# Linear attention and a gated feed-forward: one chunk more projected by block products, with the sums of its right operands on GpSimd

## The chip, the cores and the metric

One core of a Trainium2 chip runs the kernel. Its engines work side by side, each through its own list of instructions in order: TensorE (PE; its weight loads are PEld), VectorE (DVE), ScalarE (ACT), GpSimd (POOL) and SyncE (SP), which here issues the transfers. The metric is the time of one execution in microseconds on the device.

## The reference

```
q_s = softmax of q over the head's 64 columns
k_s = softmax of k over the 576 tokens of a sequence
kv  = einsum('bhsd,bhse->bhde', k_s, v)
x   = einsum('bhsd,bhde->bhse', q_s, kv), laid out as 4608 tokens x 512
out = ((x @ w_a) * (x @ w_b)) @ w_out        # w_a, w_b: 512 x 1536, w_out: 1536 x 512
```

Eight batches, eight heads, all in fp32.

## The kernel before, in words

The 4608 tokens are cut into nine chunks of 512 (`c` from 0 to 8). For each, the attention part makes x, and the feed-forward part two products, the gate (`a * b`) and the projection to the output. An fp32 product is made of three matmuls of parts: each operand is split into a high and a low part (`split` and the like: ScalarE casts the high part, VectorE subtracts it for the low one), and high x high, high x low and low x high are summed.

The 1536 columns of the gate are taken in NI = 6 pairs of blocks (`p`, and `i = pair_at(c, p)`, L1367, the pair that stands at place p). From chunk 1 on the gate of a pair goes by seven block products instead of eight (Strassen-Winograd): `product` (L848) makes each of 12 matmuls of 256 columns (L854) with weights that are sums of weight blocks (S1 to S4 and A11, A12, A22, 512 KB each), loaded again for each chunk by `get_w` (L493, SP). `last_w` keeps the weights of a chunk's last pair where the next chunk begins with the same pair.

The projection of chunks 0 to 2 is direct: `project` (L878), 144 matmuls of 512 columns for a chunk (L883), summed over all pairs in four banks, then `store`. Chunks 3 to 8 (`BY_BLOCKS = 3`) project by seven block products too: `block_step` (L1505) makes one of them, six matmuls of 256 columns (L1518). Its left operands are sums of gate blocks (`left_sums`, L1476, on VectorE), split by `split_lefts` (ScalarE L1471, VectorE L1472). Its right operands come from w_out by `right_sums(i)` (L1412), once for a pair: two sums of 512 columns (L1425) and four differences of 256 (L1431) on VectorE into y2 and t2, which are split into tiles `kept` (L1438, L1439). The kept tiles take the place of w_out's own tiles `wo`. The other right blocks are written to DRAM (`dr`) and come back through a ring of four slots by `get_right` (L1447). The pairs 0 to 4 have their right sums in chunk 2 (places 1 to 5), pair 5 at place 0 of chunk 3.

The keys of a batch are made ready by `kv_soft` (L530): VectorE takes maxima over the tile (L542 to L544, into m1), GpSimd a maximum over partitions (`partition_all_reduce`, L533, into mx), VectorE subtracts it (L565), ScalarE takes the exponential (L568), and TensorE multiplies keys and values (L603, into pk). Each is done twice for a chunk (two head groups). GpSimd also makes the sums of the gate's weights for chunk 1 (`sums`, L514).

The scheduler has no say: `ORDER` (L32) lists, for each engine, the order in which its instructions run, by their number in the program, and `in_order` (L294) makes a chain of them. An instruction that waits holds up all that stands behind it on its engine.

## Time and profile before

| | |
|---|---|
| median of 3 runs | 919.17 us (918.96 to 920.0) |
| the profiled execution | 917.98 us, span 916.2 us |
| TensorE busy | 904.6 us, 99% |
| VectorE busy | 714.4 us, 78% |
| ScalarE busy | 492.5 us, 54% |
| GpSimd busy | 113.2 us, 12% |
| moved through the SP queue | 305.16 MB |

The span is from the first to the last instruction of the profiled execution, and 1.8 us of its own time lie around it. Chunk 1 begins in the trace at 136.6 us, chunk 2 at 238.8, chunk 3 at 336.6, chunk 4 at 432.8. The page gives busy time over the whole span; how the stages differ is seen in the view by stretches, what an engine does one after the other in the timeline. The value in brackets behind a row of a timeline is how long the engine was idle just before, and who ended that.

### The profile page before, as it was taken

How to read it: one execution, taken by the hardware profiler on the slowest of the kernel's cores; microseconds unless marked ns; L12 is line 12 of the kernel's file. 1: busy time of each engine (PE TensorE's matmuls, PEld its weight loads, DVE VectorE, ACT ScalarE, POOL GpSimd, SP SyncE). 2: the span in 40 equal slices, each digit the busy share in tenths (PEclk: the TensorE clock that was granted, in tenths of full speed). 3: DMA queues.
4: the chain of work that ended last, by engine and by line, in shares of the span. 5: the costliest groups of instructions: out<-in, count | busy, mean ns of one | idle time of the engine just before them, and what ended most of it. 6: DMA issues, size and time to landing. Idle time of an engine off the chain costs nothing.

```text
span 916.2 us, 19531 instructions
## 1 busy us (share of the span) xinstructions
PE 904.6 (99%) x7155; PEld 850.2 (93%) x7155; DVE 714.4 (78%) x1557; ACT 492.5 (54%) x1350; POOL 113.2 (12%) x93
## 2 busy tenths in 40 slices
PE   7999999999999999999999999999999999999998
PEld 4677789899999999999999999999999999999997
DVE  7989999668966777679878887788877776876556
ACT  6989777555433456345735563446543655342322
POOL 3645343432100000000000000000000000000000
PEclk8999999999999999999999999999999999999999
DMA  9999999999999999999999989998999799959962
GB/s 350 380 384 367 378 369 363 365 362 341 385 350 329 361 338 322 393 322 346 333 346 350 331 301 352 324 356 306 343 323 399 247 349 326 385 189 320 347 252 93
DMA packets 124735, 306.40 MB, mean 334 GB/s; under 512 B 13408, under 2 KB 30432, under 8 KB 124640
## 3 DMA queue, kind: packets, MB, share of 16 engines
q1 hardware_dynamic: 124640, 305.16, 93.7%
q8 instruction: 57, 0.93, 0.4%
q14 instruction: 38, 0.31, 0.1%
HBM read 256.87 MB, written 48.23 MB: 333 GB/s over the span
## 4 chain that ended last, share of the span: by engine, by line
PE 89%; DMA 5%; ACT 2%; DVE 2%; issue 1%; SPq 0%; DVEq 0%; ACTq 0%
PE kx L854 30%; PE po L1518 19%; PE ky L854 15%; PE po L883 9%; PE ka L854 8%; PE pt L829 3%; PE px L785 2%; PE pk L603 2%; DMA raw<-in_w_ab 2%; DMA wo_raw<-in_w_out 1%; DMA dw<-ws 1%; DMA kt_first<-in_kt 1%; PE pl L1682 1%; DMA ws<-dw 1%; ACT wr L382 0%
## 5 line engine op out<-in xcount | busy, mean ns | idle before, releaser
L854 PE MATMUL kx<-xo,ws 128*128 128x256 f32 x2304 | 312.4, 282 | 0.0
L854 PEld LDWEIGHTS kx<-xo,ws 128*128 128x128 f32 x2304 | 292.1, 188 | 4.6 <-ACT u L1621 0.3
L854 PE MATMUL ky<-xo,ws 128*128 128x256 f32 x1152 | 157.7, 282 | 0.0
L854 PEld LDWEIGHTS ky<-xo,ws 128*128 128x128 f32 x1152 | 146.2, 188 | 0.9
L1472 DVE TENSOR_TENSOR left<-cc,left 128x256 fp32r<-128x256 f32 x245 | 96.2, 420 | 50.0 <-ACT left L1471 46.4
L1471 ACT CAST left<-cc 128x256 fp32r<-128x256 f32 x245 | 92.1, 404 | 65.8 <-DVE cc L1487 34.9
L1518 PE MATMUL po<-xo,left 128*128 128x256 f32 x750 | 106.2, 282 | 0.0
L1518 PE MATMUL po<-kept,left 128*128 128x256 f32 x720 | 100.7, 283 | 0.0
L1518 PEld LDWEIGHTS po<-xo,left 128*128 128x128 f32 x750 | 96.7, 189 | 0.4 <-issue 0.2
L1518 PEld LDWEIGHTS po<-kept,left 128*128 128x128 f32 x720 | 92.2, 189 | 0.4
L854 PE MATMUL ka<-xo,ws 128*128 128x256 f32 x576 | 80.7, 282 | 0.2 <-DMA ws<-dw 0.2
L696 ACT ACTIVATE qt<-qt,st 128x64 f32<-128x64 f32 x224 | 76.1, 342 | 6.9 <-issue 3.5
L829 PE MATMUL pt<-xo,ws 128*128 128x512 f32 x288 | 77.5, 407 | 0.1
L854 PEld LDWEIGHTS ka<-xo,ws 128*128 128x128 f32 x576 | 74.2, 188 | 1.7 <-DMA ws<-dw 0.6
L1621 ACT COPY u<-kx 128x512 f32<-128x512 f32 x48 | 28.2, 587 | 80.1 <-PE kx L854 39.1
L533 POOL PARTITION_ALL_REDUCE mx<-m x20 | 17.0, 849 | 423.0 <-DVE m L544 423.0
L829 PEld LDWEIGHTS pt<-xo,ws 128*128 128x128 f32 x288 | 53.0, 189 | 14.4 <-issue 2.6
L1487 DVE TENSOR_TENSOR cc<-cc 128x256 f32<-128x256 f32 x140 | 56.9, 420 | 1.6
L883 PE MATMUL po<-wo_w,gh 128*128 128x512 f32 x192 | 57.2, 396 | 0.0
L1607 ACT COPY u<-kx 128x512 f32<-128x512 f32 x48 | 28.1, 586 | 50.5 <-PE kx L854 50.3
L1642 ACT COPY cc<-kx 128x256 f32<-128x256 f32 x48 | 17.8, 371 | 68.5 <-PE kx L854 68.5
L1622 DVE TENSOR_TENSOR cc<-ky,u 128x512 f32<-128x512 f32 x48 | 33.0, 688 | 20.6 <-ACT u L1621 16.7
(175 smaller groups left out, 1368.2 us busy)
## 6 DMA issues: line engine op xcount, KB each, us to landing
ws<-dw SPq DMA_DIRECT2D x277, 512.0 KB, 6.6
xo<-dr SPq DMA_DIRECT2D x125, 256.0 KB, 5.6
dw<-ws SPq DMA_DIRECT2D x42, 512.0 KB, 6.8
mr<-dq SPq DMA_DIRECT2D x112, 128.0 KB, 6.6
raw<-in_w_ab SPq DMA_DIRECT2D x24, 512.0 KB, 7.6
vt<-in_v SPq DMA_DIRECT2D x28, 325.0 KB, 6.5
qt<-in_q SPq DMA_DIRECT2D x32, 256.0 KB, 5.1
kt<-in_k SPq DMA_DIRECT2D x24, 320.0 KB, 5.1
```

Source lines behind the costliest of these rows:

```text
L603: nc.tensor.matmul(pk[h * D:(h + 1) * D], kt[:, j, h], vt[:, j, h], start=(j == 0), stop=(j == J - 1),)
L696: nc.scalar.activation(out=qt[:, j, h], in_=qt[:, j, h], func=AF.Exp, bias=st[:, h, 0, j:j + 1], accum_out=st[:, h, 1, j:j + 1],)
L829: nc.tensor.matmul(pt, w[:, wp], x[g][:, xp], start=(g == 0 and i == 0), stop=(g == NP - 1 and i == 2),)
L854: ins = nc.tensor.matmul(pt[:, n], w[:, n, wp, c], x[:, xp, c], start=(first and n == 0 and i == 0), stop=(i == 5), skip_group_check=True,)
L883: nc.tensor.matmul(po[t], a[:, ts], wo[f][:, w], start=(f == 0 and i == 0), stop=(f == NF - 1 and i == 2),)
L1471: nc.scalar.copy(out=a[:, 0], in_=cc[:, n, part])
L1472: nc.vector.tensor_tensor(out=a[:, 1], in0=cc[:, n, part], in1=a[:, 0].bitcast(F32), op=ALU.subtract)
L1487: nc.vector.tensor_tensor(out=o, in0=x, in1=y, op=op)
L1518: nc.tensor.matmul(pt[:, t], x.left[:, ap, t * P:(t + 1) * P], w[:, wp], start=(first and t == 0 and n == 0), stop=(n == 2), skip_group_ch ...
L1607: nc.scalar.copy(out=u2, in_=kx)
L1621: nc.scalar.copy(out=u4, in_=kx)
L1622: nc.vector.tensor_tensor(out=cc[:, 3], in0=ky, in1=u4, op=ALU.add)
```

## The change

Chunk 2 projects by blocks as well (`BY_BLOCKS = 2`). The right sums are made on GpSimd, and earlier: pairs 0 to 2 in chunk 1 (places 2 to 4), pairs 4, 5 and 3 at the head of chunk 2 (places 0 and 1). The pairs run in reverse in every even chunk from chunk 2 on; before, in chunks 4, 6 and 8. With that chunk 1 ends with the pair chunk 2 begins with, and chunk 2 with that of chunk 3, and seven weights are kept at either boundary. All five lists of `ORDER` are replaced. The changed kernel's lines are 6 further on (L533 becomes L539, L1425 L1431, L1431 L1437), from the end of the function some more.

```diff
@@ ORDER
...
     "Pool": (
...
-        "41 44-88 "
...
+        "95 97 96 98 107-108 101-104 106 105 109-124 "
     ),
@@
-    BY_BLOCKS = 3
+    BY_BLOCKS = 2
...
     def pair_at(c, p):
-        return NI - 1 - p if c >= BY_BLOCKS and (c - BY_BLOCKS) % 2 else p
+        return NI - 1 - p if c > 0 and c % 2 == 0 else p
@@ right_sums
-            nc.vector.tensor_tensor(
+            nc.gpsimd.tensor_tensor(
                 out=y[:, r].rearrange("p a b -> p (a b)"), in0=w[:, 0], in1=w[:, 1], op=ALU.add
             )
...
         for o, x, z in ((t1, b12, b11), (t2, b22, t1), (t3, b22, b12), (t4, b21, t2)):
-            nc.vector.tensor_tensor(out=o, in0=x, in1=z, op=ALU.subtract)
+            nc.gpsimd.tensor_tensor(out=o, in0=x, in1=z, op=ALU.subtract)
@@ operand
                 if op in (A11, A12, A22):
-                    return get_w(i, op)
-                w = split_w(sy[i][op])
-                put_w(i, op, w)
+                    w = get_w(i, op)
+                else:
+                    w = split_w(sy[i][op])
+                    put_w(i, op, w)
+                if p == NI - 1 and pair_at(c + 1, 0) == i:
+                    last_w[i, op] = w
                 return w
@@ the loop over pairs
             kz = ka
+            if c == BY_BLOCKS and p == 0:
+                right_sums(NI - 2)
+                run_pending()
+                right_sums(NI - 1)
+                for _ in range(4):
+                    get_right()
+            if c == BY_BLOCKS and p == 1:
+                right_sums(NI - 3)
             multiply(kx, A11, B11, True)
...
-            if c == BY_BLOCKS - 1 and p > 0:
-                right_sums(p - 1)
+            if c == BY_BLOCKS - 1 and 2 <= p < NI - 1:
+                right_sums(p - 2)
...
-            if c == BY_BLOCKS and p == 0:
-                right_sums(NI - 1)
-                for _ in range(4):
-                    get_right()
```

The lists themselves tell a reader nothing, so three places of the orders follow, of the program before and of the changed one. `x10` is ten of a kind in a row, brackets name the engines or queues that an instruction waits for.

GpSimd around the maxima of the keys, before: the last sums for the gate's weights (L514), then an ISA row without operands, then the maxima over partitions of chunks 2 and 3 (L533).

```order
L514 TENSOR_TENSOR ws_y_2558<-ws_y_2554,ws_y_2558 128x512 [waits DMAHW2_49,Pool_49]
L514 TENSOR_TENSOR ws_y_2554<-ws_y_2560,ws_y_2554 128x512 [waits Pool_49]
L514 TENSOR_TENSOR ws_y_2556<-ws_y_2556,ws_y_2554 128x512 [waits DMAHW5_49,Pool_49]
L533 ISA
L533 ISA mx_3017<-m1_3019 128x128 [waits DVE_49]
L533 ISA mx_3026<-m1_3028 128x128 [waits DVE_49]
L533 ISA mx_3281<-m1_3283 128x128 [waits DVE_49,Pool_49]
L533 ISA mx_3290<-m1_3292 128x128 [waits DVE_49,Pool_49]
```

In the changed kernel, the same stretch: the first difference of t2_2744 (pair 2) stands ahead of the first two maxima, the rest of it and the sums of pairs 4 and 5 between them and the next two.

```order
L1437 TENSOR_TENSOR t2_2744<-y2_2743 128x256 [waits PE_49,Pool_49]
L539 ISA
L539 ISA mx_3153<-m1_3155 128x128 [waits DVE_49]
L539 ISA mx_3162<-m1_3164 128x128 [waits DVE_49]
L1437 ISA
L1437 TENSOR_TENSOR t2_2744<-y2_2743,t2_2744 128x256 [waits Pool_49]
...
L1437 TENSOR_TENSOR t2_3053<-y2_3052,t2_3053 128x256 [waits Pool_49] x2
L539 ISA
L539 ISA mx_3428<-m1_3430 128x128 [waits DVE_49]
L539 ISA mx_3437<-m1_3439 128x128 [waits DVE_49]
L1431 ISA
L1431 TENSOR_TENSOR y2_3324<-wo6_w_929 128x512 [waits DVE_49,Activation_49]
```

Where one row without operands stood in this stretch, four stand now, and 15 sums (four of 512 columns, eleven of 256) lie between the second and the third maximum. A fifth follows ahead of the maxima of chunk 4.

VectorE between the first maximum over partitions and the data of the second, before: from the subtraction of mx_3017 (L565) to the next maximum (L544), with the second subtraction at the end.

```order
L565 TENSOR_TENSOR kt_2940<-kt_2940,mx_3017 128x640
L802 TENSOR_TENSOR xt_2745<-xf_1587 128x512
L542 TENSOR_TENSOR m2_3027<-kt_2944 128x256
L543 TENSOR_TENSOR m1_3028<-m2_3027 128x128
L700 TENSOR_SCALAR st_2937<-st_2937 128x2x4
L1615 TENSOR_TENSOR cc_2763<-ka_2762,u3_2765 128x512
L544 TENSOR_TENSOR m1_3028<-m1_3028,kt_2944 128x128
```

In the changed kernel, the same stretch, from behind the subtraction of mx_3153 (kt_3012) to the maximum m1_3164 that the second all-reduce waits for.

```order
L1445 TENSOR_TENSOR kept10_2509<-t2_2496,kept10_2509 128x2x256
L366 TENSOR_TENSOR xo_2814<-xf_1587,xo_2814 128x512
L366 TENSOR_TENSOR gl1_2788<-cc_2582,gh1_2787 128x512
L1445 TENSOR_TENSOR kept11_2512<-t2_2496,kept11_2512 128x2x256
L983 TENSOR_TENSOR xf_1587<-px_2763,mr_2587 128x512
L548 TENSOR_TENSOR m2_3163<-kt_3016 128x256
L809 TENSOR_TENSOR xt_2818<-xf_1587,xt_2817 128x512
L814 TENSOR_TENSOR xt_2824<-xf_1587 128x512
L549 TENSOR_TENSOR m1_3164<-m2_3163 128x128
L707 RECIPROCAL st_3009<-st_3009 128x2x4
L706 TENSOR_SCALAR st_3009<-st_3009 128x2x4
L550 TENSOR_TENSOR m1_3164<-m1_3164,kt_3016 128x128
```

With the subtraction itself thirteen instructions stand between the two maxima, seven before.

TensorE where the keys of the next chunk are multiplied with their values, in chunk 2, before: pk_3377 stands behind the last direct projection of chunk 1 and ahead of gate products.

```order
L883 MATMUL po0_1742<-wo11_w_1513,gl1_2904 128x512
L883 MATMUL po2_1744<-wo11_w_1513,gl1_2904 128x512
L603 MATMUL pk_3377<-vt_3202,kt_3200 64x65 x10
L854 MATMUL kx_3181<-xo_2742,ws_3208 128x256 x12
L854 MATMUL ky_3182<-xo_2757,ws_3223 128x256 x12
L854 MATMUL kx_3181<-xo_2749,ws_3237 128x256 x12
L854 MATMUL ka_3183<-xo_2816,ws_3299 128x256 x6
L883 MATMUL po3_3096<-wo0_w_1522,gh0_3177 128x512 x2
```

In the changed kernel, that place: kt_3316 is the tile of keys that the third maximum, mx_3428, is subtracted from.

```order
L889 MATMUL po0_1742<-wo11_w_1513,gl1_2976 128x512
L860 MATMUL kx_3297<-xo_2826,ws_3470 128x256 x12
L860 MATMUL ka_3299<-xo_2888,ws_3446 128x256 x6
L860 MATMUL ky_3298<-xo_2829,ws_3366 128x256 x6
L609 MATMUL pk_3488<-vt_3318,kt_3316 64x65 x10
L1524 MATMUL po0_3380<-xo_3072,left_3278 128x256 x6
L609 MATMUL pk_3488<-vt_3322,kt_3320 64x65 x10
L1524 MATMUL po1_3403<-xo_3072,left_3279 128x256 x6
L1524 MATMUL po2_3462<-xo_3073,left_3280 128x256 x6
```

The block products of the projection (L1524) take the place of the direct ones in chunk 2, the first of them right behind pk_3488.

## Rows read from the trace of the kernel before

**Rows 1.** The page: busy time of each engine with its share of the span and its number of instructions (part 1), the granted clock of TensorE and the busy share of the DMA engines in tenths in 40 slices of the span (part 2), and the queue that SP feeds (part 3).

```profile
PE 904.6 (99%) x7155; PEld 850.2 (93%) x7155; DVE 714.4 (78%) x1557; ACT 492.5 (54%) x1350; POOL 113.2 (12%) x93
...
PEclk8999999999999999999999999999999999999999
DMA  9999999999999999999999989998999799959962
...
q1 hardware_dynamic: 124640, 305.16, 93.7%
```

**Rows 2.** The view by stretches, for chunks 1, 2 and 3: after the stretch and its length, the busy time of each engine with its instructions in brackets, in the order PE, PEld, DVE, ACT, POOL, then granted clock, DMA share and GB/s.

```profile
136.60:238.80 102.20, 102.05 (x781) 93.55 (x779) 80.90 (x170) 60.33 (x181) 34.24 (x24) 1.00 0.99 362
238.80:336.60 97.80, 97.80 (x729) 90.78 (x728) 71.99 (x146) 40.40 (x87) 3.40 (x4) 1.00 0.98 348
336.60:432.80 96.20, 96.20 (x835) 94.16 (x834) 75.91 (x179) 49.73 (x139) 3.41 (x4) 1.00 0.99 348
```

**Rows 3.** The tile ws, the weights of the gate's products: one of the lines on what its engines were idle for, with the time in us and the number of times.

```profile
  DMA ws<-dw: 0.7, 2
```

**Rows 4.** The timeline of TensorE in three short stretches of chunks 1 to 3: start, time from the first start to the last end of the group, line, operation, tiles, shape, number. Each group starts where the one before it has made its last start, so starts give the pitch.

```profile
237.45 1.39 PE L603 MATMUL pk<-vt,kt 128*64 128x65 f32 x40
238.76 1.10 PE L854 MATMUL kx<-xo,ws 128*128 128x256 f32 x7
...
245.15 1.55 PE L883 MATMUL po<-wo_w,gh 128*128 128x512 f32 x6
246.53 0.87 PE L883 MATMUL po<-wo_w,gl 128*128 128x512 f32 x3
247.24 0.88 PE L854 MATMUL kx<-xo,ws 128*128 128x256 f32 x6
...
358.98 2.30 PE L1518 MATMUL po<-xo,left 128*128 128x256 f32 x18
361.11 1.59 PE L854 MATMUL kx<-xo,ws 128*128 128x256 f32 x12
```

**Rows 5.** The groups of instructions by line and by form over the whole span: out<-in, shape, count, then busy us, mean ns of one, and the idle time before them with what ended most of it.

```profile
L1472 DVE TENSOR_TENSOR left<-cc,left 128x256 fp32r<-128x256 f32 x245 | 96.2, 420 | 50.0 <-ACT left L1471 46.4 <-PE ka L854 2.9
...
L1471 ACT CAST left<-cc 128x256 fp32r<-128x256 f32 x245 | 92.1, 404 | 65.8 <-DVE cc L1487 34.9 <-DVE cc L1623 12.1 <-PE po L1518 9.6
...
L514 POOL TENSOR_TENSOR ws_y<-ws_y 128x512 f32<-128x512 f32 x24 | 35.2, 1465 | 46.3 <-DMA ws_y<-dy 31.0 <-DVE xf L977 7.6 <-DMA mr<-dq 6.2
...
L568 ACT ACTIVATE kt<-kt 128x640 f32<-128x640 f32 x24 | 17.7, 738 | 18.8 <-DVE kt L565 17.8 <-DMA xo<-dr 1.0
...
L533 POOL PARTITION_ALL_REDUCE mx<-m x20 | 17.0, 849 | 423.0 <-DVE m L544 423.0
L360 DVE TENSOR_TENSOR gl<-cc,gh 128x512 fp32r<-128x512 f32 x24 | 16.9, 708 | 10.4 <-PE po L883 5.8 <-ACT gh L357 4.4
L360 DVE TENSOR_TENSOR xo<-xf,xo 128x512 fp32r<-128x512 f32 x24 | 16.6, 691 | 0.0
...
L565 DVE TENSOR_TENSOR kt<-kt,mx 128x640 f32<-128x640 f32 x20 | 16.3, 816 | 1.0 <-POOL mx L533 0.9
...
L360 DVE TENSOR_TENSOR ws<-wy,ws 128x512 fp32r<-128x512 f32 x18 | 16.0, 888 | 2.3 <-ACT ws L357 2.3
...
L1425 DVE TENSOR_TENSOR y<-wo_w 128x512 f32<-128x512 f32 x12 | 8.0, 684 | 0.0
...
L1431 DVE TENSOR_TENSOR t<-y,t 128x256 f32<-128x256 f32 x12 | 5.0, 420 | 0.1
```

**Rows 6.** The page's DMA issues: number, KB of each, and the median us from issue to landing.

```profile
ws<-dw SPq DMA_DIRECT2D x277, 512.0 KB, 6.6
xo<-dr SPq DMA_DIRECT2D x125, 256.0 KB, 5.6
```

**Rows 7.** The instructions of line 533 on GpSimd's queue: the row of the change of its configuration, with duration in ns, first and last start.

```profile
L533 POOLq MODIFY_POOL_CONFIG  x2: 13/13/13, 212.3 to 212.3; - x2
```

**Rows 8.** The same for line 1175, GpSimd's first sum of the run.

```profile
L1175 POOLq MODIFY_POOL_CONFIG  x2: 4/4/4, 1.5 to 1.5; - x2
```

**Rows 9.** The timeline of GpSimd around its last sums for the gate's weights and its first maximum over partitions.

```profile
205.26 6.80 POOL L514 TENSOR_TENSOR ws_y<-ws_y 128x512 f32<-128x512 f32 x4 [7.57 <-DVE xf L977]
224.13 1.05 POOL L533 PARTITION_ALL_REDUCE mx<-m  x1 [12.07 <-DVE m L544]
```

**Rows 10.** The timeline of VectorE from the maximum that the all-reduce of 224.13 waited for, and on into the stretch in which the second one is made ready.

```profile
223.71 0.29 DVE L544 TENSOR_TENSOR m<-m,kt 128x128 f32<-128x128 f32 x1
...
228.25 0.82 DVE L565 TENSOR_TENSOR kt<-kt,mx 128x640 f32<-128x640 f32 x1
228.98 0.69 DVE L802 TENSOR_TENSOR xt<-xf 128x512 f32<-128x512 f32 x1
231.15 0.43 DVE L542 TENSOR_TENSOR m<-kt 128x256 f32<-128x256 f32 x1 [1.48 <-DMA kt<-in_k]
...
233.29 0.68 DVE L977 TENSOR_TENSOR xf<-px,mr 128x512 f32<-128x512 f32 x1
233.90 0.68 DVE L1622 TENSOR_TENSOR cc<-ky,u 128x512 f32<-128x512 f32 x1
234.49 0.81 DVE L565 TENSOR_TENSOR kt<-kt,mx 128x640 f32<-128x640 f32 x1
```

**Rows 11.** The timeline of GpSimd at the start of the run.

```profile
10.48 1.05 POOL L1175 TENSOR_TENSOR qts<-qts,qst 128x512 f32<-128x512 f32 x1 [9.03 <-DVE qst L1169]
```

More of the change, by code (lines that the diff above doesn't have):

```diff
@@ L179 @@
         "70 98 79 100 93 137 92 99 103 101 138 80 102 112 95 220 116 113 109-111 153 108 119 117 128 120 "
[64 rows of a table removed]
[66 rows of a table added]
     ),
     "Pool": (
-        "0-7 10 12 8-9 11 13-16 18 17 19 21-22 24 20 25 23 27 26 28 30 29 31-34 36 35 37 40 39 38 42-43 "
-        "41 44-88 "
[3 rows of a table added]
     ),
```

463 rows, old and new, of the table ORDER are left out of this document.

## The prediction

> **What bounds the kernel now.** I read the page's busy times first. TensorE is busy for 99% of the span, at a granted clock of 0.9 or more in all slices but the first, which is the 2.4 GHz level [rows 1]. DMA is nearly as full, GpSimd has little to do. So the question is what TensorE has to do and where it could be made to wait. The stretches by chunk say the same of the place of the change: in chunk 2 (238.8 to 336.6) TensorE is busy for 97.80 of 97.80 us, and chunk 3, which already projects by blocks, takes 96.20 with more instructions [rows 2]. VectorE, 72 to 81 us of each, has room; a transfer of gate weights held TensorE up for 0.7 us in the whole run [rows 3]. A saving on TensorE is therefore a saving of time, as long as no new wait appears.
>
> **TensorE's own work.** In chunk 2, 144 matmuls of 512 columns (L883) go and 252 of 256 columns (L1518) come. From start to start, nine of L883 take 247.24 - 245.15 = 2.09 us, 0.2322 each; eighteen of L1518 take 361.11 - 358.98 = 2.13, 0.1183 each [rows 4]. 144 x 0.2322 = 33.4; 252 x 0.1183 = 29.8. **Saving 3.6 us.** The stretches of chunks 2 and 3 differ by 1.6 only, but they hold different amounts of attention work beside the products; I take the count.
>
> **VectorE and ScalarE.** Chunk 2 gains 42 left operands (ScalarE 42 x 404 ns = 17.0, VectorE 42 x 420 = 17.6), 24 sums of lefts (24 of the same width, 10.1) and some ten snapshots and sums of output banks (about 7.5, estimated at 0.7 each), and loses 12 low parts of gates (12 x 708 = 8.5) [rows 5]. Of the right sums' 18 us on VectorE (L1425 8.0 and L1431 in two halves of 5.0) five sixths, 15, lay in chunk 2 and go to GpSimd. VectorE there: 72.0 + 17.6 + 10.1 + 7.5 - 8.5 - 15 = 84 of some 94 us. ScalarE: 40 + 17 - 12 x 0.62 = 50. Both stay below TensorE, so this costs nothing; the cover is the ten us that VectorE is left with.
>
> **Transfers.** Fourteen loads of 512 KB go (the seven weights of a pair are kept at each of the two boundaries), 22 of right blocks of 256 KB come (18 for Q1 to Q3 and four for the first pair): 1.5 MB less of 305 [rows 1]. The SP queue is passed with no step later than a product needs it: ahead of each gate product in chunk 2 there are now fewer bytes, not more. I cost it at nothing; without that cover one late block costs its landing, 5.6 us [rows 6].
>
> **GpSimd.** It gets 12 sums of 512 and 24 of 256 columns. A 512 sum there takes 1465 ns on average [rows 5], a half one I estimate at 0.73, so 35 us, all in chunks 1 and 2, where it has 34 and 3 us of work [rows 2]. As throughput that is nothing. As a sequence it is the one thing that worries me. The first sum t2_2744 stands ahead of the all-reduces of the maxima of chunk 2's keys, the rest between those and the all-reduces of the next keys, and at each change of kind GpSimd's order has an ISA row without operands. The trace before has that twice: as MODIFY_POOL_CONFIG, 13 ns, at 212.3 ahead of the first all-reduce [rows 7], and at 1.5 ahead of the first sum [rows 8]. The changed order has three more on one chain. What such a **change of code, R,** costs before the first call can start isn't shown, since both times GpSimd had nothing to do anyway: the all-reduce of 224.13 starts 0.13 us after VectorE's maximum is done (223.71 + 0.29), the sum of 10.48 when VectorE releases it [rows 9, 10, 11]. That bounds R: at least 0, at most 10.48 - 1.5 = 9.0 (the other gap, 11.8, is wider). If R is anything, it is something brought in, and the nearest rows for that are the landings of transfers in these stretches, 5.6 to 6.6 us in a DMA system that is 0.98 to 1.00 busy [rows 2, 6]. I take **R = 7**, a little over the larger of these, and keep 0 and 9.0 for the range.
>
> The trace shows the first call itself starting 0.13 us after its input. The Trainium skill (GPSIMD Engine Reference, 2.1 Instruction dispatch) says that the first call to freshly loaded code pays about 6 us more, 5.95 measured, with no instruction to be seen, and to budget for it. That price is taken up under the second rival.
>
> The chain, from where TensorE finishes kx_2832's first product (t2_2744's first subtraction waits for it): that subtraction 0.73, R, all-reduce 0.85 [rows 5], then VectorE must do thirteen instructions in its order before the second maximum is complete. Seven are of 512 columns, 0.60 from start to start (233.29 to 233.90 to 234.49); the subtraction from the keys takes 0.73 (228.98 - 228.25), the three maxima 0.43 + 0.29 + 0.29, the two small ones about 0.1 each: 6.1, or 7.0 with nothing overlapped; I take 6.5 [rows 10]. Then the second all-reduce 0.85, R, four sums of 512 and eleven of 256: 4 x 1.465 + 11 x 0.73 = 13.9, R, all-reduce 0.85, VectorE's subtraction 0.82 (L565), ScalarE's exponential 0.74 (L568), and TensorE's pk_3488 may start. Sum: 0.73 + 0.85 + 6.5 + 0.85 + 13.9 + 0.85 + 0.82 + 0.74 = 25.2, plus 3R.
>
> TensorE's work between the same two points, counted in its order: 216 matmuls of the gate (256 columns), 52 of the direct projection, 20 of kv and six px: 216 x 0.1183 + 52 x 0.2322 + 20 x 0.033 (forty take 238.76 - 237.45 = 1.31) + about 0.9 = 39.3 [rows 4]. pk_3488 stands in TensorE's order ahead of the first block matmul; nothing behind it can pass. So the **new wait is 25.2 + 3R - 39.3 = 3R - 14.1**: none up to R = 4.7, 6.9 us at R = 7, 12.9 at 9.0. What queues behind it on VectorE are the lefts of pair 0, directly behind the two subtractions from the keys: they cost a fraction of a microsecond more, which I leave out. The first all-reduce has its own consumer, pk_3214, about 11 us of TensorE work after kx_2832 against 3.1 + R: no wait. The later switch, for pair 3's sums, has over 20 us.
>
> **Sum.** Against the profiled execution, 917.98 with a span of 916.2: -3.6 + 6.9 = +3.3, so 921.3. The median of the runs is 919.17, 1.19 higher, so **922.5**. A change under 0.2%, 1.84 us, can't be told from none; that makes 917.3 to 921.0 "no change", in R 5.3 to 6.5.
>
> **Rivals.**
> *The switches are short or early (the other side).* R is below 4.7, or the code is fetched while GpSimd still runs its sums. For it: in both switches of the trace the first call came straight after its input, and an instruction of 13 ns is all that is shown [rows 7, 9]. Against it: in both there were 9 to 12 us to hide in, and the new ones have none, since each stands between two pieces of ready work. Then only the saving is left: 919.17 - 3.6 = 915.6 (915.1 to 916.1, with the medians of single matmuls in place of the pitch). It decides at R = 5.9, where 3R - 14.1 is 3.6. Chance 0.28.
>
> *Draw.* R lies between 4.7 and 6, about the landings of 256 KB transfers: at 5.6 the wait is 2.7 and the time 918.3; from 915.6 to 919.5 over the case. Chance 0.16. By the 5.95 us of the Trainium skill (GPSIMD Engine Reference, 2.1) the wait would be 3.8 and the time 919.3; the trace so far neither shows such a price nor rules it out.
>
> *VectorE pays for GpSimd's sums.* VectorE's 512-wide instructions average 888 ns in the opening stretch, where GpSimd works too, against 691 later for the same width [rows 5]. At 30% more over the 35 us in which GpSimd is busy, VectorE has some 10 us more to do in two chunks with 94 and 102 us and 84 to 85 of work. Against it: TensorE ran through the stretches in which GpSimd did its sums for chunk 1 without a gap (102.05 of 102.20 busy, with 34 us of GpSimd) [rows 2]. Price: the backlog behind pk_3488 isn't made up, 3 us on top of the forecast, 925.5. Chance 0.04.
>
> *The rest comes late*: the block order's first right operands, four loads at the head of chunk 2, or kept tiles that wait for the old weights' last use. One landing, 5.6, in place of the stall: 921.2. Nor would the change then do what it says, save TensorE time. Chance 0.02.
>
> **Numbers.** The forecast, R from 6 to 9: 0.50; its own range 919.5 to 928.5, its likeliest time 922.5. Faster: the first rival and the draw up to R = 5.3, 0.28 + 0.05 = 0.33. Same: the rest of the draw, 0.11, and the forecast from 6 to 6.5, 0.06: 0.17. Slower: 0.44 + 0.04 + 0.02 = 0.50. The range must reach the first rival's 914.9 and R = 8.7 (3R - 14.1 = 12.0): 914.9 to 927.6.
>
> **What would show it.** In the changed profile: five more MODIFY_POOL_CONFIG stretches on GpSimd and gaps of about 7 us, with nothing released by another engine, on either side of the all-reduces near 225 and near 262; a hole in TensorE of about 7 us just ahead of L609 some 24 us into chunk 2, and no other hole; chunks 3 to 8 unchanged to a few tenths; 144 fewer L889 and 252 more L1524 at the same pitch. Wrong it would be if the gaps on GpSimd were under 5 us (then TensorE shows no hole and the end comes 3.6 earlier), or if the hole stood at a block matmul behind a left or a transfer.

## The result, and the profile after

The changed kernel takes **934.21 us** (932.43 to 935.21, 4 runs) where the kernel before, on the same chip, took 919.07: a ratio of **1.0147, 95% interval 1.0122 to 1.0171**, 15 us slower. 922.5 had been forecast, and 914.9 to 927.6 as the range. The profiled executions, 932.43 (span 930.6) and 917.98 (916.2), are apart by the same 14.4.

The page of the changed kernel, the lines of [rows 1], with the shares by engine of the chain that ended last (part 4):

```profile
PE 908.2 (98%) x7263; PEld 855.6 (92%) x7263; DVE 730.4 (78%) x1586; ACT 498.9 (54%) x1380; POOL 153.0 (16%) x129
...
q1 hardware_dynamic: 126304, 303.58, 92.3%
...
PE 75%; DMA 13%; DVE 6%; ACT 3%; issue 1%; SPq 1%; POOL 0%; DVEq 0%; ACTq 0%; POOLq 0%
```

TensorE holds the 108 more matmuls that were counted. In the kernel before the chain ran over TensorE for 89% and over transfers for 5%; now for 75% and 13%. Chunks 1 to 3 by stretches, as [rows 2] (after the length: PE, PEld, DVE, ACT, POOL, then granted clock, DMA share, GB/s):

```profile
133.70:247.30 113.60, 107.57 (x769) 95.97 (x768) 88.17 (x170) 64.91 (x201) 55.51 (x41) 0.98 0.96 345
247.30:347.40 100.10, 97.92 (x840) 94.11 (x839) 83.34 (x173) 51.40 (x133) 24.68 (x25) 1.00 0.97 338
347.40:445.70 98.30, 97.03 (x871) 96.00 (x871) 75.92 (x178) 44.49 (x122) 2.87 (x4) 1.00 1.00 348
```

Chunk 2 was to become shorter. Chunk 1 is 11 us longer, chunk 2 longer by 2, and even chunk 3, in which nothing was to change, by 2, with its transfers at a share of 1.00.

**The switches.** GpSimd around its all-reduces, where [rows 9] showed it in the kernel before:

```profile
224.17 0.73 POOL L1437 TENSOR_TENSOR t<-y 128x256 f32<-128x256 f32 x1 [2.72 <-PE kx L860]
234.43 0.72 POOL L539 PARTITION_ALL_REDUCE mx<-m  x1 [9.53 <-issue]
241.20 1.06 POOL L539 PARTITION_ALL_REDUCE mx<-m  x1 [6.05 <-DVE m L550]
249.23 0.98 POOL L1437 TENSOR_TENSOR t<-y,t 128x256 f32<-128x256 f32 x1 [6.97 <-issue]
...
263.61 1.59 POOL L1437 TENSOR_TENSOR t<-y,t 128x256 f32<-128x256 f32 x2
271.29 1.43 POOL L539 PARTITION_ALL_REDUCE mx<-m  x2 [6.09 <-DVE cc L1493]
```

The two gaps "<-issue" are the price R: 9.53 and 6.97 us in which nothing that the profile shows held GpSimd up. The maximum for the all-reduce of 234.43 was complete at 224.07, so with its input ready only the change of code is left for it to wait for. The gap ahead of 271.29 is a third R, 6.09 us, though the profile puts it down to VectorE: the sums ended at 265.20, the first maximum was complete before that, at 264.54, and the second at 269.29. VectorE and TensorE at these places, the first answering to [rows 10]:

```profile
223.78 0.29 DVE L550 TENSOR_TENSOR m<-m,kt 128x128 f32<-128x128 f32 x1
...
235.18 0.83 DVE L571 TENSOR_TENSOR kt<-kt,mx 128x640 f32<-128x640 f32 x1 [5.15 <-POOL mx L539]
235.93 0.69 DVE L1445 TENSOR_TENSOR kept<-t,kept 128x512 fp32r<-128x512 f32 x1
236.53 0.68 DVE L366 TENSOR_TENSOR xo<-xf,xo 128x512 fp32r<-128x512 f32 x1
237.13 0.69 DVE L366 TENSOR_TENSOR gl<-cc,gh 128x512 fp32r<-128x512 f32 x1
...
263.83 0.71 DVE L550 TENSOR_TENSOR m<-m,kt 128x128 f32<-128x128 f32 x1
...
269.01 0.28 DVE L550 TENSOR_TENSOR m<-m,kt 128x128 f32<-128x128 f32 x1
```

```profile
234.84 0.63 PE L889 MATMUL po<-wo_w,gh 128*128 128x512 f32 x2
237.87 0.50 PE L889 MATMUL po<-wo_w,gl 128*128 128x512 f32 x1 [2.40 <-DVE gl L366]
239.12 0.98 PE L609 MATMUL pk<-vt,kt 128*64 128x65 f32 x20 [0.74 <-DVE xf L983]
...
244.38 1.70 PE L860 MATMUL kx<-xo,ws 128*128 128x256 f32 x12 [1.11 <-ACT u L1638]
...
273.92 0.80 PE L609 MATMUL pk<-vt,kt 128*64 128x65 f32 x20 [1.01 <-ACT kt L574]
```

VectorE stands in front of the subtraction from the keys (L571) for 5.15 us. Three places behind it is the low part of a gate, gl1_2788, and TensorE's *projection of chunk 1* wants that. So most of the wait falls not on the products of keys and values that the chain was followed to (pk_3488, at 273.92, waits 1.01), but earlier, on a product that has nothing to do with keys. In the 4 us of the hole TensorE is busy for 1.39, at a granted clock of 0.95; in the next 4 the clock is 0.62, so part of them lies at the lower level, 1.2 GHz. The transfers run thin meanwhile: SP's next load of keys waits 5.2 us for products of keys (pk) that L571 held up, since it fills the tile that they read (the view by stretches; the next fence is the SP queue):

```profile
236.00:240.00 4.00, 1.39 (x21) 1.01 (x21) 4.00 (x9) 1.73 (x7) 0.00 (x0) 0.95 0.80 307
240.00:244.00 4.00, 3.27 (x9) 2.15 (x7) 3.71 (x9) 2.77 (x7) 1.06 (x1) 0.62 0.71 234
```

```profile
234.08 0.80 SPq L1430 DMA_DIRECT2D dr<-wo_w  x1
240.17 0.33 SPq L527 DMA_DIRECT2D kt<-in_k  x1
```

SP issues nothing for 5.3 us; behind that load stand those of the weights. Later, between 314 and 791 us, TensorE waits for weights, five times instead of twice and for 2.4 us instead of 0.7 [rows 3]:

```profile
PE kx L860 <- DMA ws<-dw: 1.7, 4, 0.7
...
PE ky L860 <- DMA ws<-dw: 0.7, 1, 0.7
```

**Where the time lies.** For each kernel I gave every matmul the pitch that its width has undisturbed (0.231 us for 512 columns, 0.119 for 256, and so on: the 40th percentile over equal neighbours) and took as lost what TensorE's starts fall behind the running sum. The sums are 875.4 before and 872.0 after, a saving of 3.4 of work. Lost time, by how much of that work has been done (100 is reached at 129 us of the kernel before, in late chunk 0; 200 at 232, near the end of chunk 1; 240 at 272):

```
                                        0-100  100-200  200-240  240-end
before                                   29.0      2.6      0.7      4.5
after                                    28.4      5.9     10.7      9.5
after minus before                       -0.6     +3.3    +10.0     +5.0   = 17.7; 17.7 - 3.4 = 14.3
```

That is the 14.4 of the spans but for rounding. The columns depend a little on the pitch that the narrow matmuls are given; their differences between kernels move by no more than about half a us with it. The first column lies between 27.9 and 31.5 over the kernels of these tables, with no order in it that I can see; I read it as chance. The second is in the main chunk 1, the third the boundary of chunks 1 and 2 and what follows to 272 us, the fourth the larger part of chunk 2 and chunks 3 to 8. These three are the three questions for the experiments.

### The profile page after: what moved, and what is told of

The parts are those of the page before. It is cut to its first block, busy times and chain, and to the rows that moved or that the text cites. A ratio compares the mean times of both kernels' runs of the same rounds, so it can differ in the third digit from the quotient of the medians.

```text
span 930.6 us, 19868 instructions
## 1 busy us (share of the span) xinstructions
PE 908.2 (98%) x7263; PEld 855.6 (92%) x7263; DVE 730.4 (78%) x1586; ACT 498.9 (54%) x1380; POOL 153.0 (16%) x129
## 3 DMA queue, kind: packets, MB, share of 16 engines
q1 hardware_dynamic: 126304, 303.58, 92.3%
## 4 chain that ended last, share of the span: by engine, by line
PE 75%; DMA 13%; DVE 6%; ACT 3%; issue 1%; SPq 1%; POOL 0%; DVEq 0%; ACTq 0%; POOLq 0%
PE kx L860 24%; PE po L1524 19%; PE ky L860 12%; PE ka L860 6%; PE pt L835 5%; PE po L889 4%; DMA mr<-dq 4%; DMA ws<-dw 3%; PE pk L609 2%; PE px L791 1%; ACT qt L702 1%; DMA raw<-in_w_ab 1%; DVE xo L366 1%; DMA wo_raw<-in_w_out 1%; DMA xo<-dr 1%
## 5 line engine op out<-in xcount | busy, mean ns | idle before, releaser
L1478 DVE TENSOR_TENSOR left<-cc,left 128x256 fp32r<-128x256 f32 x287 | 112.6, 420 | 52.6 <-ACT left L1477 46.8
L1477 ACT CAST left<-cc 128x256 fp32r<-128x256 f32 x287 | 107.6, 404 | 66.6 <-DVE cc L1493 35.8
L1524 PE MATMUL po<-xo,left 128*128 128x256 f32 x882 | 126.3, 283 | 0.0
L1524 PE MATMUL po<-kept,left 128*128 128x256 f32 x840 | 118.5, 282 | 0.0
L1524 PEld LDWEIGHTS po<-xo,left 128*128 128x128 f32 x882 | 114.3, 189 | 0.4
L1524 PEld LDWEIGHTS po<-kept,left 128*128 128x128 f32 x840 | 108.1, 189 | 0.3
L539 POOL PARTITION_ALL_REDUCE mx<-m x20 | 15.6, 785 | 382.5 <-DVE m L550 366.9
L835 PE MATMUL pt<-xo,ws 128*128 128x512 f32 x288 | 75.4, 404 | 0.1
L1493 DVE TENSOR_TENSOR cc<-cc 128x256 f32<-128x256 f32 x164 | 66.9, 421 | 2.0
L1638 ACT COPY u<-kx 128x512 f32<-128x512 f32 x48 | 28.1, 586 | 75.1 <-DVE cc L1632 38.7
L1619 ACT COPY u<-kx 128x512 f32<-128x512 f32 x48 | 28.0, 584 | 45.6 <-PE kx L860 45.6
L1624 ACT COPY u<-kx 128x512 f32<-128x512 f32 x48 | 28.0, 583 | 38.9 <-PE kx L860 38.5
```

The costliest lines, as they stand in the source:

```text
L835: nc.tensor.matmul(pt, w[:, wp], x[g][:, xp], start=(g == 0 and i == 0), stop=(g == NP - 1 and i == 2),)
L1477: nc.scalar.copy(out=a[:, 0], in_=cc[:, n, part])
L1478: nc.vector.tensor_tensor(out=a[:, 1], in0=cc[:, n, part], in1=a[:, 0].bitcast(F32), op=ALU.subtract)
L1493: nc.vector.tensor_tensor(out=o, in0=x, in1=y, op=op)
L1524: nc.tensor.matmul(pt[:, t], x.left[:, ap, t * P:(t + 1) * P], w[:, wp], start=(first and t == 0 and n == 0), stop=(n == 2), skip_group_ch ...
L1619: nc.scalar.copy(out=u3, in_=kx)
```

## The experiments

All ratios are to the kernel before on the same chip, with a 95% interval; 1 us is 0.0011.

**1. The switches away.** The first four maxima over partitions become products:

```diff
+        if len(maxima) <= 4:
+            nc.gpsimd.tensor_tensor(out=mx, in0=m1, in1=ones, op=ALU.mult)
+        else:
             nc.gpsimd.partition_all_reduce(...)
```

> The changed kernel with the same five orders; only the maxima over partitions of the keys of chunks 2 and 3 (four all-reduces) are replaced by an elementwise product with ones of 128x128 on GpSimd, so that GpSimd keeps one code through chunks 1 and 2 (this leaves out the maximum over partitions of these keys). Theory A, the three changes of code on the chain are the cause: the holes at 235 to 245 and 272 go (about 10 us by the count of pitches), and what the SP queue lost behind them; 920 to 924. Theory B, GpSimd's sums slow VectorE and the new order is worse as such: the changes of code matter little, over 929.

Measured **1.0059 (1.003 to 1.0087)**, against 1.0147: the switches cost about 8 us, and without them the kernel is still 5 us over before, where the saving should have shown. The time, 925.65, lies between the two theories. The three gaps are gone with the changes of code: GpSimd's products start within 0.1 us of their maximum or of the end of GpSimd's own work, and the sums follow them at once.

**2. The right sums on VectorE**, at the same places of the order (both sums `nc.gpsimd` to `nc.vector`):

> The changed kernel with the right sums back on VectorE, at the places in time that they had on GpSimd; TensorE, ScalarE and SP keep their orders. No change of code is left in chunks 1 and 2. Theory A: as without changes of code, 918 to 923, if VectorE (84 + 8 us of 95 in chunk 2) keeps up; up to 926 if not. Theory B: less than the kernel without changes of code on GpSimd by several us, since GpSimd's sums are gone as well.

**1.0091 (1.006 to 1.0123)**. No switch is left in a tight place here either, and again no gain; neither theory had expected 927.35.

**3. Part of the sums on GpSimd**, with the whole computation kept:

```diff
+        on = nc.gpsimd if i < 2 else nc.vector
-            nc.gpsimd.tensor_tensor(
+            on.tensor_tensor(
```

> The changed kernel with the right sums of pairs 0 and 1 alone on GpSimd (chunk 1, ahead of all maxima), those of pairs 2 to 5 on VectorE at the same places in time: one change of code in place of four, hidden as before, and no GpSimd beside VectorE at the chunks' boundary. The whole computation. Theory A and C: the holes at 235 to 245 and 272 go and VectorE has to make 10 us more in chunk 2: 920 to 925. Theory D: 927 or more.

**1.0056 (1.003 to 1.0082)**, the best form of the change with the whole computation, and slower than before; 925.77 again lies between the theories. Lost time by the four columns: 31.5, 4.1, 3.7, 6.9. Against after, 7.0 of the 10.0 at the boundary are gone, and 2.6 of the 5.0 behind it. GpSimd's sums beside VectorE at the boundary went with the switches here; it is experiment 1 that took away the switches alone.

**4. The order mended.** In the lists, L571 of kt_3012 goes behind the second maximum, its products to a later place, and L571 of kt_3316 with its products some 100 matmuls later:

```diff
@@ VectorE
-L571 kt_3012   (ahead of L1445, L366 gl1_2788, ...)
 ...
 L550 m1_3164
+L571 kt_3012
```

> The changed kernel, only the places of a few instructions moved: VectorE's subtraction from kt_3012 behind the maxima of the second head group (12 instructions later), its exponential and its ten matmuls behind the direct projection of that place; the subtractions from kt_3316 and kt_3320, their exponentials and their twenty matmuls some 100 matmuls later. The changes of code stay. Theory A, with the price in what queues behind the wait: most of 10 us comes back, 923 to 927. A variant of it, the changes of code cost TensorE time as such (through transfers or VectorE): 930 or more. Theory B: 931 or more.

**1.019 (1.0168 to 1.0212)**: slower still, where theory A had expected most of 10 us back. R is unchanged (9.65, 7.01 and 6.01 us), and the waits only move: TensorE waits for ScalarE's u (3.0 and 1.8), acc (3.2) and ot (1.6). VectorE while GpSimd does its sums (the timeline of VectorE):

```profile
246.37 0.41 DVE L1633 TENSOR_TENSOR cc<-cc 128x256 f32<-128x256 f32 x1
...
248.73 1.51 DVE L1664 TENSOR_TENSOR cc<-cc 128x256 f32<-128x256 f32 x1
```

The same form takes 0.41 and 1.51. A wait that is shared by three engines is not removed by moving one instruction.

**5. GpSimd's sums alone**, in the kernel before (its right sums `nc.vector` to `nc.gpsimd`, nothing else), and **6.** the same with its first seven maxima as products:

> The kernel before, with one part of the change alone: the right sums on GpSimd, at the same places in time (chunk 2 places 1 to 5, chunk 3 place 0), all other orders as before. GpSimd then changes its code in chunk 2 between the sums and the maxima of the keys of chunks 3 and 4. Theory A: a few us more than before, 920 to 925, with holes where a maximum follows a sum closely. Theory B: VectorE slower by GpSimd's 35 us, 921 to 924 without such holes. Neither: 917 to 919.5.

> The kernel before with the right sums on GpSimd, and the maxima over partitions of the keys of chunks 2 to 4 (six, and a seventh) replaced by the product with ones, so that no change of code is left among the sums (it leaves these maxima out). Theory A: the 27 us by which that part alone was slower are the changes of code; without them 919 to 923. Theory C adds: VectorE loses in chunk 2 by GpSimd's sums what it gains by not making them, so not under 918.5. If the changes of code are not it: 935 or more.

**1.0293 (1.0266 to 1.032)** and **1.003 (1.0009 to 1.0051)**. Moving work to an engine that is 12% busy costs 27 us, where 925 was the most that either theory expected, and some 25 of them are the changes of code. GpSimd in the first of the two, and TensorE at the time of the first gap:

```profile
254.98 0.72 POOL L532 PARTITION_ALL_REDUCE mx<-m  x1 [8.03 <-issue]
...
324.80 0.71 POOL L1430 TENSOR_TENSOR t<-y,t 128x256 f32<-128x256 f32 x1 [11.87 <-issue]
...
373.84 0.72 POOL L532 PARTITION_ALL_REDUCE mx<-m  x1 [8.10 <-issue]
```

```profile
259.24 1.65 PE L853 MATMUL kx<-xo,ws 128*128 128x256 f32 x6 [8.00 <-ACT u L1620]
```

The first of these R comes out as a hole of its own length; behind the second TensorE stands for 3.7 and 1.5 us, behind the third for 5.7.

**7. No right sums at all**: experiment 1 with the 36 sums as memsets.

> The kernel without changes of code in chunks 1 and 2, and besides that the 36 right sums on GpSimd replaced by writes of zeros of the same tiles at the same places in its order (it leaves out the right sums and the maximum over partitions of the keys of chunks 2 and 3). Theory C, what is left of the loss without changes of code (4.7 us over the kernel before, where 3.3 less were due) is GpSimd's sums slowing VectorE's instructions of two inputs, 0.69 us to between 1.0 and 1.8: 916 to 920, and VectorE's rows near 240 to 260 back at 0.69. Theory D, it is the new order and the transfers: 923 or more.

**1.0106 (1.0059 to 1.0153)**. Theory C, that GpSimd's *new* sums are what is left, fell. But the trace shows the old ones at it: GpSimd at 203 us, with sums for the gate's weights that the kernel before has too, then VectorE, then TensorE:

```profile
202.98 4.90 POOL L520 TENSOR_TENSOR ws_y<-ws_y 128x512 f32<-128x512 f32 x3 [5.17 <-DVE cc L1668]
...
208.35 1.82 POOL L520 TENSOR_TENSOR ws_y<-ws_y 128x512 f32<-128x512 f32 x1
```

```profile
199.69 0.68 DVE L366 TENSOR_TENSOR ws<-ws_y,ws 128x512 fp32r<-128x512 f32 x1
...
204.97 1.78 DVE L366 TENSOR_TENSOR gl<-cc,gh 128x512 fp32r<-128x512 f32 x1
206.66 1.76 DVE L366 TENSOR_TENSOR ws<-ws_y,ws 128x512 fp32r<-128x512 f32 x1
...
208.95 0.41 DVE L1661 TENSOR_TENSOR cc<-kx,cc 128x256 f32<-128x256 f32 x1
209.29 0.68 DVE L990 TENSOR_TENSOR xf<-px,mr 128x512 f32<-128x512 f32 x1
```

```profile
209.42 2.14 PE L867 MATMUL kx<-xo,ws 128*128 128x256 f32 x12 [1.90 <-DVE cc L1661]
```

Two subtractions that take 0.68 alone take 1.78 and 1.76 beside the sums, so L1661 is late and TensorE stands for 1.9 us. L1661 and L990, which read one operand from PSUM, are not slowed beside the sum of 208.35. The second column varies with how the sums fall beside VectorE's work (a reading that no run tests): over the kernel before it is +3.3 in after, but +6.7, +8.5 and +6.1 in the profiles of experiments 1, 2 and 7, and +1.5 in that of experiment 3.

**8 to 10. Room for the transfers.** Each later load of gate weights brings its first half only, and the products use that half twice; in the kernel before, in experiment 3, and in the changed kernel:

```diff
-        last_w["load"] = nc.sync.dma_start(out=w.bitcast(F32), in_=dw[i, op].bitcast(F32))
+        last_w["load"] = nc.sync.dma_start(out=w[:, 0].bitcast(F32), in_=dw[i, op][:, 0].bitcast(F32))
...
-                        pt[:, n], w[:, n, wp, c], x[:, xp, c],
+                        pt[:, n], w[:, 0, wp, c], x[:, xp, c],
```

> The kernel before, in which every later load of gate weights (ws, 277 of 512 KB) brings only its first half, 256 KB, and the gate's products use that half for both of their column blocks: same instructions on every engine, about 71 MB of 305 less to move; the gate's values are those of one half. The profile of the kernel before shows transfers at 0.98 to 1.00 busy through chunks 1 to 3, but only 0.7 us in which TensorE waited for such a load. Both theories: 0 to 2 us faster than before, 918 to 921. It is the basis for the two others of this call.

> The changed kernel with the right sums of pairs 0 and 1 on GpSimd and those of pairs 2 to 5 on VectorE (no GpSimd change of code in a tight place), with the same halved loads. With whole loads it took 1.0056 of before, about 5 us more. Theory T (the lost saving is a matter of transfers: these run full in chunks 1 to 3, the new order of loads starts some later, and what is late there can't be made up): with room in the transfers the saving of 3.3 shows, 3 to 4 us under the kernel before with halved loads. Theory V (VectorE, nearly full at the end of chunk 1, and the new order of the engines' work itself): transfers don't matter, 4 to 6 us over the kernel before with halved loads.

> The changed kernel itself with the same halved loads. Theory T: only the two changes of code at the head of chunk 2 and the saving are left, 3 to 5 us over the kernel before with halved loads (about the 3.3 of the forecast). Theory V: 12 to 14 us over it, as with whole loads.

**1.001 (0.9994 to 1.0026)**, **1.0058 (1.0035 to 1.0082)**, **1.012 (1.0091 to 1.0148)**. Half loads alone gain nothing, where up to 2 us had been expected. By the totals theory V holds for the split, 4 us over its basis (the kernel before with the same half loads); after is 9 over it where it was 15, between the two theories. The columns show why: each theory is right for a stretch of its own.

```
                                        0-100  100-200  200-240  240-end
before, half loads                       28.9      7.5      0.7      3.9
split, half loads                        28.6     10.4      3.6      3.5
after, half loads                        28.0     10.5     10.2      3.6
```

Behind the boundary all three lose the same, 3.5 to 3.9, where before and after had 4.5 and 9.5: the late losses were transfers. At the boundary nothing is gained, and in chunk 1 all three lose 4.6 to 6.3 more than with whole loads. Half loads bring that on only where GpSimd has its sums for the gate's weights: in the next two experiments these are gone as well, and that column is at 1.9 and 2.2.

**11 and 12. The old sums away too**: the 24 sums for the gate's weights become memsets, in experiment 7 and in the kernel before, both with half loads.

```diff
-            nc.gpsimd.tensor_tensor(out=a[o], in0=a[x], in1=a[y], op=op)
+            nc.gpsimd.memset(a[o], 1.0)
```

> The changed kernel with three things taken out at once: the first four maxima over partitions are products on GpSimd (no change of code near chunk 2), the 36 right sums are memsets, and the 24 sums on GpSimd for the gate's weights (ws_y, 1.5 us each, in chunks 0 and 1) are memsets too, so that hardly a sum on GpSimd is left beside VectorE's work in chunk 1; and the gate's weights come by halves, as in the two runs before. What it computes differs in all that. In the run with only the first two taken out (1.0106 of before) VectorE's 512-wide instructions beside sums of ws_y took 1.78 instead of 0.68, and TensorE waited 1.9 for one of them at 207. Theory S (what eats the saving is GpSimd's sums beside a VectorE that the new order leaves little room, and the transfers): 3 to 4 us under the kernel before with the same two things taken out. Theory O (the new order of the engines' work itself costs it): 0 to 5 over it.

> The basis: the kernel before with the 24 sums on GpSimd for the gate's weights as memsets and the gate's weights by halves; its right sums and maxima as they were. Theory S: it gains a little too, 0 to 3 us from before, since the profile of before shows VectorE's 512-wide instructions at 888 ns in the opening stretch. Theory O: the same.

**0.9944 (0.9927 to 0.9961)** and **0.9943 (0.9923 to 0.9963)**: level. The basis gains 5 to 6 us on before, the changed order, from 1.0106, 12 to 15. Theory S had the saving show here, 3 to 4 us under the basis; it doesn't.

**13 to 15.** The same with whole loads, in experiment 7, in the kernel before and in experiment 3, to tell the sums from the transfers:

> The changed kernel with right sums as memsets, the first four maxima over partitions as products, and the 24 GpSimd sums for the gate's weights as memsets; the gate's weights are loaded whole. Only the loads differ from the run that stood level with the kernel before in the same trim. Theory S1 (the sums on GpSimd carried it): within 2 us of the kernel before without those 24 sums. Theory S2 (the transfers carried it): 4 to 8 us over it.

> The basis: the kernel before with the 24 GpSimd sums for the gate's weights as memsets, whole loads. With halved loads as well it took 0.9943 of before, with halved loads alone 1.001. S1: 0.993 to 0.996. S2: 0.997 to 1.0.

> The changed kernel with the right sums of pairs 0 and 1 on GpSimd and those of pairs 2 to 5 on VectorE, and the 24 GpSimd sums for the gate's weights as memsets; whole loads. With those 24 sums it took 1.0056 of before. S1: 0 to 3 us over the kernel before without those sums. S2: as with them, 4 to 6 over it.

**1.0012 (0.9994 to 1.0031)**, **0.9974 (0.9956 to 0.9991)**, **1.0001 (0.9991 to 1.001)**: experiments 13 and 15 are 3.1 and 2.8 us over their basis (14), where the same two were 7 to 10 and 5 over before. Of the ranges, 2.8 lies in S1's, 3.1 between the two, and the basis in S2's. So the sums carried the larger part, and the transfers a smaller one:

```
                                        0-100  100-200  200-240  240-end
before, no weight sums                   28.8      2.6      0.8      6.1
split, no weight sums                    28.4      3.0      3.6      8.2
no right sums, no weight sums            27.9      3.3      3.8      8.1
no right or weight sums, half loads      28.9      2.2      3.2      3.5
before, no weight sums, half loads       29.4      1.9      0.8      3.9
```

Without the sums chunk 1 loses what it lost before. With half loads on top the end does too. What stays is 200-240: 2.4 more than the basis with no switch, no sum and no late load (experiment 11), 2.8 to 3.0 with whole loads. One part of it is VectorE, which works almost without a break from 223 to 235 us, so that L1637 comes late, behind it ScalarE's u, and TensorE starts 1.0 us behind its pitch (experiment 13, VectorE, then TensorE):

```profile
234.62 0.68 DVE L1637 TENSOR_TENSOR cc<-ka,u 128x512 f32<-128x512 f32 x1
```

```profile
236.03 1.69 PE L867 MATMUL kx<-xo,ws 128*128 128x256 f32 x12 [0.82 <-ACT u L1643]
```

In the stretch from 220 to 240 VectorE is busy for 18.19 of 20 us there, for 19.37 in experiment 3, for 17.57 in the kernel before. The other part is in TensorE's own order. The products of keys and values stand in five groups there (experiment 13), where the kernel before has two, the 40 of [rows 4] and 20 at 254.62:

```profile
232.58 0.80 PE L616 MATMUL pk<-vt,kt 128*64 128x65 f32 x20
...
246.93 0.57 PE L616 MATMUL pk<-vt,kt 128*64 128x65 f32 x12
...
251.84 0.45 PE L616 MATMUL pk<-vt,kt 128*64 128x65 f32 x8
...
263.38 0.80 PE L616 MATMUL pk<-vt,kt 128*64 128x65 f32 x20
...
265.50 0.80 PE L616 MATMUL pk<-vt,kt 128*64 128x65 f32 x20
```

At every group, in both kernels, four starts come 0.07 to 0.12 us late, two as it begins and two behind its end, together 0.4 us; three groups more are 1.2 us. With the 1.0 of the wait that is nearly the whole of the 2.4. That this order costs it is read from the trace; no run puts the groups together again.

## Why the prediction was wrong

**The saving** of 3.6 was right as work: 3.4 by the running sums. It shows nowhere as time: the changed order comes out at best level with its basis (experiments 11, 12). What ate it, and 14 us more, are three terms, one sized too small and two put at nothing.

**The switches.** The chain that the prediction followed is there, and it is what TensorE waits for at the boundary. From t2_2744's first subtraction (224.17) to pk_3488 (273.92) it takes 49.8 us: 9.5 + 7.0 + 6.1 = 22.6 for the three R, where 3 x 7 = 21 was taken, and 27.2 for the rest, where 25.2 was taken; of the 2.0 more, 2.1 are GpSimd's 15 sums, 16.0 for 13.9. Against the 39.3 of TensorE's work that is a wait of 10.5, not 6.9, and the column shows 10.0. Taking the switches away gives back 7.0 of it (experiment 3) and about 8 us of the whole time (experiment 1), because 2.4 to 3.0 are lost there without them, too; the two losses overlap and don't add up. That 7.0 looks like the 6.9 of the forecast is luck.

R = 7 was a choice between bounds of 0 and 9.0, and the upper bound, drawn from the start of the run, was too low: 9.5 here, 11.9 in experiment 5. The rivals with short switches are out; only the two last changes, behind the all-reduces of 271.29 and ahead of those of chunk 4, were hidden. The Trainium skill (GPSIMD Engine Reference, 2.1 Instruction dispatch) gives 5.95 us for the first call to freshly loaded code; the shortest gaps here, 6.01 and 6.09, are near that, the others are longer, and the return to an ordinary sum pays as well.

The step "the first all-reduce has its own consumer, pk_3214 ... no wait" failed as to the place: what is queued behind a waiting instruction on VectorE was named for the second switch only, and the first held up gl1_2788. SP's load, queued behind the tile of the same keys, wasn't seen at all. Two slips of the working change nothing: the trace has four changes of configuration more than before, not five, and the lower bound of 914.9 isn't the 915.1 of the rival that it is said to reach.

**"Transfers ... I cost it at nothing"** is the step that failed by the largest single amount, +5.0 from the middle of chunk 2 on, where "a few tenths" stood. Fewer bytes was right (303.58 MB for 305.16). But the transfers run nearly full in chunks 1 to 3 (a share of 0.96 to 1.00), and what is late there came back as waits for weights up to hundreds of us later; with half loads it is gone. About half of it is the held SP queue (2.6 less without the switches, experiment 3). Where the other half starts, with fewer bytes to move and no queue held, stays open.

**"Both stay below TensorE, so this costs nothing"** failed beside it. The mean was right: VectorE is busy for 83.3 us in chunk 2, where 84 was forecast. But the work that comes in stands at the boundary, where before it had 2.4 of 20 us free, and the one wait of 1.0 us in experiment 13 is of that. Larger is what the rival "VectorE pays for GpSimd's sums", at 0.04, names: it makes chunk 1 slow, by 1.5 to 8.5 us in the profiles with the weight sums (+3.3 in after), by 0.4 and 0.7 once these are memsets. It was priced for the new sums alone, at the place of the second switch; but the new order makes the old sums expensive too (they cost the kernel before 2.4 us and the split 5). The argument against it, that TensorE ran through chunk 1 without a gap beside 34 us of GpSimd, held for the order before, which left VectorE room. How VectorE's instructions take the sums (the groups by form: before and experiment 12, then after and experiment 11):

```profile
L360 DVE TENSOR_TENSOR ws<-ws_y,ws 128x512 fp32r<-128x512 f32 x24 | 18.6, 788 | 0.8 <-ACT ws L357 0.8
```

```profile
L360 DVE TENSOR_TENSOR ws<-ws_y,ws 128x512 fp32r<-128x512 f32 x24 | 16.1, 683 | 0.8 <-ACT ws L357 0.8
```

```profile
L366 DVE TENSOR_TENSOR gl<-cc,gh 128x512 fp32r<-128x512 f32 x12 | 12.1, 1006 | 4.2 <-ACT gh L363 4.1
```

```profile
L366 DVE TENSOR_TENSOR gl<-cc,gh 128x512 fp32r<-128x512 f32 x12 | 8.3, 688 | 6.2 <-ACT gh L363 6.1
```

Memsets in the place of sums, at the same point of GpSimd's queue, leave VectorE at its clean 683 to 688 ns. The Trainium skill (SBUF — State Buffer, Who interferes with whom) has the rule: a VectorE instruction with both inputs in SBUF contends with a GpSimd instruction that reads SBUF, not with one that only writes it, and the loser waits for the whole of the other. The runs agree: beside memsets the subtractions keep their 0.68, xf<-px,mr, whose px lies in PSUM, keeps it beside a sum, and 1.78 is about 0.68 and the rest of a sum that was already running (4.90 for three, 1.6 each). Since a memset is also shorter than a sum, these runs take away GpSimd's own time together with the contention; that it is the contention that TensorE waits for is shown, for one wait, by the rows of 204.97 to 209.42. A mean of 30% more, as in the prediction, hides that single instructions take 2.6 times as long, and one late one is what TensorE waits for.

So of +14.4 in the profiled pair: -3.4 work (forecast -3.6), +10.0 at the boundary, the chain of the switches (forecast 6.9), +3.3 in chunk 1, GpSimd's sums beside VectorE (forecast 0), +5.0 transfers (forecast 0), of which the switches bring half, and -0.6 by chance. The split rests on one profile each; the sum of the four columns is exact, the shares are good to about 1 us, and that of chunk 1 less so, as the spread from 1.5 to 8.5 shows.

**What stays open.** Whether another order at the boundary would give back the 1.0 us of VectorE's wait and the 1.2 of the split groups: the one order that was tried (experiment 4) was made for the switches, and it was slower.

## What to carry to other kernels

Before work goes to GpSimd, list what its queue alternates between: each change of kind between ready pieces cost 6 to 12 us here, and whatever stands behind the first reader *in that reader's queue* pays, not only the data's own consumer. Read the room of a helper engine from the 20 us in which the new work falls, not from the mean of a stage, and count instructions with two operands in SBUF beside GpSimd's sums at their worst, not their mean. Where transfers run nearly full, what a held queue loses is paid later, in a place whose code did not change. A gap that the profile puts down to another engine is worth a look at when the input was ready.

## What the runs showed of the hardware that was not expected

A change of code on GpSimd between a maximum over partitions and ordinary sums costs 6.01 to 11.87 us where no idle time hides it, in both directions. VectorE's instructions of 256 and 512 columns with both operands in SBUF went from 0.41 and 0.68 to as much as 1.51 and 1.78 us beside GpSimd's sums, and stayed at 0.68 beside its memsets. A group of narrow products (65 columns, on 64 columns of the array) between wide ones cost TensorE 0.4 us at its two ends (two groups before, five in experiment 13). After 4 us in which TensorE was busy for 1.39, the granted clock of the next 4 us was 0.62.
